# Fused delta-rule attention and two MLP layers on one core: new priorities at the start, no filling matmuls, layer 2 in groups of four

## The chip, the core and the metric

The kernel runs on one core of a Trainium2 chip. The metric is the device time of one execution in microseconds; the kernel before took 1034.82 us, the median of three runs (1033.31 to 1038.89).

## What is computed

Inputs are q, k and v of shape (4, 8, 768, 48) (batch, heads, sequence, head dimension), beta of shape (4, 8, 768), and two pairs of weights, 384 x 2048 and 2048 x 384, all float32. The reference, cut:

```python
k_n = k / (norm(k) + 1e-6)
for t in range(S):                               # per batch and head
    y[t] = q[t] @ state
    state += beta[t] * outer(k_n[t], v[t] - k_n[t] @ state)
x = y.transpose(0, 2, 1, 3).reshape(3072, 384)   # tokens x (head, dim)
h = x @ w_in                                      # layer 1
x = where(h >= 1, h, where(h <= -1, 0, (h + 1)**2 / 4)) @ w_out
h = x @ w2_in                                     # layer 2
out = (h * clip(h + 3, 0, 6) / 6) @ w2_out
```

## The kernel before

The sequence is cut into 12 chunks of 64 positions. Within a chunk the recurrence becomes matrix work: products K K' and K Q', the inverse of a unit triangular matrix, and multiplications with the state that is carried to the next chunk. All 32 heads are done together. Per chunk the steps are: `load_tok` or `load_blocks` (keys and queries), `norms`, `transposes` on TensorE or `block_transposes` on VectorE, `products` (L575), `inverse` (L634), and `chain` (L766), which gives the outputs y and the next state. y is written to the tile XB, the input of layer 1. For the first four chunks (`b16`) the inverse goes in 15 steps over rows of 16, each a multiplication (L661, out TMP) and a subtraction (L666, out TL) that depends on it; then come four multiplications on TensorE. The tuple `tpool` says for which chunks these steps run on GpSimd (1 to 11); the others use VectorE. `ct` says from which chunk on VectorE transposes instead of TensorE.

Layer 1 works on blocks: chunk 0, chunk 1 (256 tokens each), then pairs of chunks (512 tokens). A unit of a block is one of 16 slices f of the hidden dimension. `mlp_h` (L992) makes the hidden slice. To keep float32 precision each operand is split into a high and a low part, so it has three times three matmuls (9), the weights stationary and XB moving. ScalarE and VectorE then apply the activation in GF and split the result into GH (high) and GL (low). `mlp_o` (L1018) multiplies these with the output weights: 9 matmuls in layer 1, 12 in layer 2, where GH and GL are stationary and the weights (384 columns) move. The weights arrive in raw form and are split by `wload` (L909): per half slice two instructions on ScalarE or VectorE (out TBS), a merge (L953), a high copy to WLA and a subtraction (L376). Layer 2 takes blocks of 512 tokens, its GH and GL have two buffers each, and it issues the outputs of unit f right after the hidden part of unit f + 1. `fin2` evacuates and stores a block's four output tiles.

Nothing runs in the order of the code. `Plan.op` collects the instructions with a duration, dependences and a priority; `Plan.emit` simulates the engines and picks, for each, the instruction that can start first, and among equals the lower priority number. Attention of chunk c has priority c plus an entry of the table `PR` (L360), the weight splits `wl` + `wls` f, the activations `MP`, TensorE's MLP work 50 with a turn rule (`RATIO`). Where several engines can do a step, the planner takes the one that ends first. While nothing of the MLP can run, `fill` lets the planner put matmuls without use (GH on itself, 128 x 512) into TensorE's idle time. Emitted so, each engine runs its own list in order, and the names of tiles in the views carry no chunk.

## Time and profile before

| | |
|---|---|
| median of three runs | 1034.82 us |
| profiled execution | 1037.03 us, its span 1035.2 us |
| TensorE busy | 986.5 us (95%) in 11941 matmuls |
| VectorE, ScalarE, GpSimd busy | 610.3, 531.8, 286.7 us |
| mean granted TensorE clock | 0.984 |
| chain that ended last | TensorE 77%, VectorE 6%, DMA 5%, ScalarE 5%, issue 2% |
| matmuls without use | 73, of them 3 open a sum |

The span is the time from the first to the last instruction; the time of the execution has some 2 us around it. TensorE busy counts a matmul from its start to its modelled end, so a stream of overlapping matmuls reads as 100% even where each stands a little longer than its columns need. For such stretches the distance of starts says more than the busy time.

### The profile page before, as it was taken

Reading aid. Unit: us, or ns where it says so; the run is one execution under the profiler, and the core shown is the slowest. Engines: PE = TensorE matmul, PEld = TensorE weight load, DVE = VectorE, ACT = ScalarE, POOL = GpSimd, SP = SyncE. Lnnn points to the kernel's source line nnn. Section 1 sums busy time; section 2 is a strip of 40 time slices with the busy share of each in tenths; the row PEclk is TensorE's granted clock in tenths of the full one; section 3 lists DMA queues with packets and bytes.
Section 4 is the critical chain, followed back from the end, with each engine's and each line's share of the span. In section 5 each row is a group of like instructions: output and inputs, shape, how many; then the busy total and the mean of one; then the engine's idle time right before and its main releaser. Section 6 shows DMA issues by size and latency. Waiting matters only on the chain.

```text
span 1035.2 us, 28435 instructions
## 1 busy us (share of the span) xinstructions
PE 986.5 (95%) x11941; PEld 841.0 (81%) x11941; DVE 610.3 (59%) x1175; ACT 531.8 (51%) x1102; POOL 286.7 (28%) x689
## 2 busy tenths in 40 slices
PE   6777898999999999999999999999999999999998
PEld 5656887877867777877888788999999999999997
DVE  4888876776877777778546797333333333333333
ACT  5789674565645646467456896232333232323322
POOL 1151503376685876865810000000000000000000
PEclk9888999999999999999999999999999999999999
DMA  6983524341243324321223753120020020200000
GB/s 132 247 196 67 105 39 78 50 70 35 39 86 62 57 38 96 56 48 30 71 68 111 252 184 91 33 62 31 1 92 0 27 67 1 92 1 1 31 1 31
DMA packets 212688, 71.84 MB, mean 69 GB/s; under 512 B 159184, under 2 KB 208464, under 8 KB 212560
## 3 DMA queue, kind: packets, MB, share of 16 engines
q1 hardware_dynamic: 212560, 70.03, 28.6%
q8 instruction: 93, 1.52, 0.6%
q14 instruction: 35, 0.29, 0.1%
HBM read 53.68 MB, written 14.16 MB: 66 GB/s over the span
## 4 chain that ended last, share of the span: by engine, by line
PE 77%; DVE 6%; DMA 5%; ACT 5%; POOL 3%; issue 2%; SPq 2%; DVEq 0%; POOLq 0%; ACTq 0%
PE bank L418 77%; DMA RAWL<-in_moe_w_in_dram 2%; DMA KN<-in_k_dram 1%; DMA E<-in_v_dram 1%; POOL TL L666 1%; POOL TMP L661 1%; DVE GF L1009 1%; SPq L446 1%; ACT GF L1007 1%; DMA ST<-in_k_dram 1%; SPq L929 0%; ACT TBS L950 0%; ACT GF L1008 0%; DMA RAWR<-in_moe_w_in_dram 0%; DVE XB L1052 0%
## 5 line engine op out<-in xcount | busy, mean ns | idle before, releaser
L418 PE MATMUL bank<-XB,WLA 128*128 128x512 f32 (+1 forms) x1404 | 334.2, 380 | 14.5 <-DVE GF L1009 9.9
L418 PEld LDWEIGHTS bank<-XB,WLA 128*128 128x128 f32 x1404 | 248.1, 188 | 64.5 <-DVE GF L1009 14.1
L376 DVE TENSOR_TENSOR GL<-GF,GH 128x512 fp32r<-128x512 f32 (+1 forms) x208 | 137.0, 660 | 87.9 <-PE bank L418 64.6
L387 ACT ACTIVATE GH<-GF 128x512 fp32r<-128x512 f32 (+1 forms) x207 | 123.5, 597 | 126.3 <-DVE GF L1013 69.3
L1013 DVE SCALAR_TENSOR_TENSOR GF<-GF,bank 128x512 f32<-128x512 f32 x96 | 66.0, 688 | 192.4 <-ACT GF L1012 192.3
L1012 ACT ACTIVATE GF<-bank 128x512 f32<-128x512 f32 x96 | 57.4, 598 | 203.1 <-PE bank L418 202.3
L661 POOL TENSOR_TENSOR TMP<-TL,DL 128x126 f32<-128x126 f32 (+25 forms) x293 | 115.2, 393 | 70.4 <-DVE DL L719 33.2
L666 POOL TENSOR_TENSOR TL<-TL,TMP 128x126 f32<-128x126 f32 (+25 forms) x293 | 120.9, 413 | 22.7
L418 PE MATMUL bank<-GH,WLA 128*128 128x512 f32 (+1 forms) x504 | 120.3, 370 | 2.4 <-issue 1.6
L418 PE MATMUL bank<-WLA,GH 128*128 128x384 f32 x576 | 113.2, 338 | 0.0
L418 PE MATMUL bank<-XB,WLB 128*128 128x512 f32 (+1 forms) x468 | 110.8, 378 | 0.6 <-ACT SM L520 0.6
L418 PEld LDWEIGHTS bank<-WLA,GH 128*128 128x128 f32 x576 | 103.7, 188 | 6.3
L1007 ACT ACTIVATE GF<-bank 128x512 f32<-128x512 f32 (+1 forms) x112 | 59.9, 535 | 84.7 <-PE bank L418 79.4
L418 PEld LDWEIGHTS bank<-GH,WLA 128*128 128x128 f32 x504 | 86.9, 192 | 18.9 <-issue 1.7
L1009 DVE SCALAR_TENSOR_TENSOR GF<-bank,GF 128x512 f32<-128x512 f32 (+1 forms) x112 | 68.3, 611 | 49.0 <-ACT GF L1008 37.8
L418 PEld LDWEIGHTS bank<-XB,WLB 128*128 128x128 f32 x468 | 82.8, 188 | 15.5 <-issue 0.8
L418 PE MATMUL bank<-GL,WLA 128*128 128x512 f32 (+1 forms) x252 | 65.4, 367 | 1.0 <-issue 0.6
L1008 ACT ACTIVATE GF<-GF 128x512 f32<-128x512 f32 (+1 forms) x112 | 63.4, 567 | 2.1
L418 PE MATMUL bank<-WLA,GL 128*128 128x384 f32 x288 | 61.5, 334 | 0.0
L418 PEld LDWEIGHTS bank<-GL,WLA 128*128 128x128 f32 x252 | 43.9, 190 | 8.9 <-issue 0.8
L418 PEld LDWEIGHTS bank<-WLA,GL 128*128 128x128 f32 x288 | 51.0, 188 | 0.0
L418 PE MATMUL bank<-GH,WLB 128*128 128x512 f32 (+1 forms) x168 | 39.6, 366 | 1.5 <-ACT GH L387 1.5
(149 smaller groups left out, 1170.2 us busy)
## 6 DMA issues: line engine op xcount, KB each, us to landing
XB<-X SPq DMA_DIRECT2D x36, 256.0 KB, 4.5
X<-XB SPq DMA_DIRECT2D x30, 256.0 KB, 2.5
KQ<-in_moe_w_in_dram SPq DMA_DIRECT2D x16, 384.0 KB, 3.9
KQ<-in_moe_w_out_dram SPq DMA_DIRECT2D x16, 384.0 KB, 4.2
KN<-in_k_dram SPq DMA_DIRECT2D x24, 192.0 KB, 3.6
RAWL<-in_moe_w_out_dram SPq DMA_DIRECT2D x12, 384.0 KB, 5.3
out_dram<-E SPq DMA_DIRECT2D x24, 192.0 KB, 1.9
RAWL<-in_moe_w_in_dram SPq DMA_DIRECT2D x24, 144.0 KB, 4.3
```

What stands on the lines that cost most here:

```text
L376: alts[e] = (d, lambda e=e: ENG[e].tensor_tensor(out=val(out), in0=val(in0), in1=val(in1), op=op))
L387: lambda: nc.scalar.activation(out=val(out), in_=val(in_), func=AF.Copy, scale=scale))
L418: nc.tensor.matmul(o, l, r, start=start, stop=stop, skip_group_check=skip)
L446: P.dma(lambda ap=ap, dst=dst: nc.sync.dma_start(out=dst, in_=ap), CH * H, CH * DM * 4, w=[("st", i, b)], r=[("st", i)], prio=pri(c, "tok" ...
L661: P.op(te, d, lambda t=t, s=s, r0=r0, a0=a0, a1=a1, m=m: ve.tensor_tensor(out=t[:, a0:a1], in0=TL[:, r0 + a0:r0 + a1, s:s + 1].to_broadcas ...
L666: P.op(te, d, lambda t=t, s=s, r0=r0, a0=a0, a1=a1: ve.tensor_tensor(out=TL[:, r0 + a0:r0 + a1, 0:s], in0=TL[:, r0 + a0:r0 + a1, 0:s], in1 ...
L1007: P.op("act", da, lambda: nc.scalar.activation(out=gf, in_=ps, func=AF.Relu, scale=0.5, bias=0.5), r=hkeys(hb, hv), w=gk, prio=MP)
L1008: P.op("act", da + 48, lambda: nc.scalar.activation(out=gf, in_=gf, func=AF.Square), w=gk, r=gk, prio=MP)
L1009: P.op("dve", 1.06 * n + 60, lambda: nc.vector.scalar_tensor_tensor(out=gf, in0=ps, scalar=1.0, in1=gf, op0=ALU.max, op1=ALU.min), r=hkeys ...
L1012: P.op("act", da, lambda: nc.scalar.activation(out=gf, in_=ps, func=AF.Relu, scale=1.0 / 6.0, bias=0.5), r=hkeys(hb, hv), w=gk, prio=MP)
L1013: P.op("dve", 1.06 * n + 60, lambda: nc.vector.scalar_tensor_tensor(out=gf, in0=gf, scalar=1.0, in1=ps, op0=ALU.min, op1=ALU.mult), r=hkey ...
```

## The change

The table of priorities and bounds is replaced. In it, chunks 0 to 3 get an own offset (`off`), the activations of the two small blocks too (`mb`), `fill` is 0 (no filling matmuls), `tpool` begins with 3, so the inverses of chunks 1 and 2 also run their steps on VectorE, `ct` is 4, so chunk 3 is transposed on TensorE, and `dg` lets the subtraction that makes GL run on GpSimd. The planner knows when a bank was last read by another engine (`Bank.free`), charges more for weight DMAs, and starts SyncE at 700 ns. A small Sqrt on ScalarE is placed first. In layer 2, from the second block on, the hidden parts of four units are emitted in a row and then the outputs of the four units before; for that GH and GL get eight buffers, the six new pairs in tiles that attention no longer uses. The last four units of the program are issued output tile by output tile, each with its evacuation and store behind it.

```diff
-RATIO = 0.213
+RATIO = 0.2479
-PR = dict(slots=2, fast=(0,), ... hm=0.0, kv=-2.522, tok=-1.749, ... fill=3000,
-          tpool=tuple(range(1, 12)), hc=2, ... mp=0, hyst=4058, ... urg=('inv', 's'), ct=3, dg=('dve',), ...)
+PR = dict(off=(1.917, 0.131, -0.844, -0.839), mb=(-0.814, -1.017), ... hm=-28.571, kv=-2.564, tok=-2.155, ... fill=0,
+          tpool=(3, 4, 5, 6, 7, 8, 9, 10, 11), hc=0, ... mp=0.167, hyst=1146.21, ... urg=('inv', 's', 'u', 'y'), ct=4, dg=('dve', 'pool'), ...)
...
+    def free(self, e):
+        return 0.0 if self.last[0] in (None, e) else self.last[1]
...
+        free["sp"] = 700.0
...
+                    if o["uses"] and e != "pe":
+                        t = max([t] + [b.free(e) for b in o["uses"]])
...
-        return c + PR[name] - (PR["first"] if c == 0 else 0)
+        return c + PR[name] - (PR["first"] if c == 0 else 0) + (PR["off"][c] if c < len(PR["off"]) else 0)
...
+    P.op("act", 1500, lambda: nc.scalar.activation(out=SM[:, 0, 0:1], in_=GF[0][:, 0:1], func=AF.Sqrt), r=[("gf", 0, 0)], w=["sm0"], prio=-31)
...
-                  cost={48: 620.0, 16: 310.0}.get(rows))
+                  cost={48: 760.0, 16: 380.0}.get(rows, 1310.0))
...
+        mp = MP + (PR["mb"][blk] if layer == 1 and blk < len(PR["mb"]) else 0)
...
-            P.op("pe", KT * (n * 0.4515 + 1), pe, r=xkeys + wkeys(f, (0,), wh), ...)
+            P.op("pe", KT * (n * 0.443 + 1), pe, r=xkeys + wkeys(f, (0,), wh), ...)
...
+        gj = n_glob % NG2 if layer == 2 else gi
+        gl, gh = (lambda x=x: x[gj][:, c0:c0 + n] for x in (GL, GH))
...
-    def fin2(bi, cs):
+    def fin2(bi, cs, ts=range(4)):
...
+    GRP, NG2 = 4, 8
...
+        for nm, n_ in (("KN0", 1), ("KN1", 1), ("ST", 2), ("X", 2), ("DL", 2), ("TL", 1), ("NH", 1), ("LT", 1), ("YS", 1)):
+            t = pool.tile([128, n_, 512], F32R, name="G2" + nm, tag=nm)
...
+    def last_outs(group):
+        bi = group[0][1]
+        cs = blocks2[bi]
+        for t in range(4):
+            bt = banks[OB2[t]]
+            def pe(t=t, bt=bt):
+                for _, _, f, _, n_ in group:
+                    for step, (wh, g) in enumerate(((0, GH), (1, GH), (0, GL))):
+                        mm(bt[:, 0:DM], g[n_ % NG2][:, t * 128:(t + 1) * 128], wl(f, wh, DM, 2 * DM), start=False, stop=f == NF - 1 and step == 2)
...
+            fin2(bi, cs, [t])
...
-            a = seq[-2]
-            mlp_o(*a)
...
+            if i == 0 or f % GRP == GRP - 1:
+                while len(seq) - done > (1 if i == 0 else GRP):
+                    out2()
...
+    while done < len(seq) - GRP:
+        out2()
+    last_outs(seq[done:])
```

On TensorE in layer 2 the kernel before has one unit's outputs (into the banks 100, 101, 102 and 95, from GH or GL) behind one hidden part (`128x512 x9`, from XB):

```order
L418 MATMUL bank_102<-WLA,GL_69 128x384
L418 MATMUL bank_95<-WLA,GL_69 128x384
L418 MATMUL bank_99<-XB_2396,WLA 128x512 x9
L418 MATMUL bank_100<-WLA,GH_70 128x384
L418 MATMUL bank_101<-WLA,GH_70 128x384
L418 MATMUL bank_102<-WLA,GH_70 128x384
```

At the same place the changed kernel has, with G2ST and G2X as two of the new buffers:

```order
L427 MATMUL bank_102<-WLA,G2ST 128x384
L427 MATMUL bank_95<-WLA,G2ST 128x384
L427 MATMUL bank_98<-XB_2695,WLA 128x512 x9
L427 MATMUL bank_99<-XB_2695,WLA 128x512 x9
L427 MATMUL bank_96<-XB_2695,WLA 128x512 x9
L427 MATMUL bank_97<-XB_2695,WLA 128x512 x9
L427 MATMUL bank_100<-WLB,G2X 128x384
L427 MATMUL bank_101<-WLB,G2X 128x384
```

Four hidden parts stand together now, and 48 output matmuls behind them; over layer 2 the changes between the two kinds fall from 187 to 69.

On VectorE, in chunk 0's inverse (steps L661 and L666, in the changed file L671 and L676), the kernel before has, beside chunk 1's norms (SM), weight splits (RAWL, TBS):

```order
L661 TENSOR_TENSOR TMP<-TL,DL 128x48
L948 TENSOR_SCALAR TBS<-RAWL 128x384
L666 TENSOR_TENSOR TL<-TL,TMP 128x4x12
L519 TENSOR_SCALAR SM<-SM 128x16
L661 TENSOR_TENSOR TMP<-TL,DL 128x55
L948 TENSOR_SCALAR TBS<-RAWL 128x384
L666 TENSOR_TENSOR TL<-TL,TMP 128x5x11
L953 SCALAR_TENSOR_TENSOR TBS<-TBS 128x384
L661 TENSOR_TENSOR TMP<-TL,DL 128x60
```

The same steps in the changed kernel:

```order
L671 TENSOR_TENSOR TMP<-TL,DL 128x48
L532 TENSOR_TENSOR SM<-SM 128x16
L676 TENSOR_TENSOR TL<-TL,TMP 128x4x12
L533 TENSOR_TENSOR SM<-SM 128x16
L671 TENSOR_TENSOR TMP<-TL,DL 128x55
L534 TENSOR_SCALAR ND_89<-SM 128x16
L676 TENSOR_TENSOR TL<-TL,TMP 128x5x11
L536 RECIPROCAL SM<-ND_89 128x16
L671 TENSOR_TENSOR TMP<-TL,DL 128x60
```

The neighbours of the steps are chunk 1's norms now; most weight splits have moved behind the inverse. From the first step to the last 31 other instructions stood between them, and 20 do now.

On TensorE around the end of that inverse (its first product is NH,GF), the kernel before has filling matmuls on GH:

```order
L418 MATMUL bank_102<-KQ 64x64 x2
L418 MATMUL bank_99<-GH_70 128x512 x49
L418 MATMUL bank_95<-NH,GF_67 32x32 x64
L418 MATMUL bank_99<-GH_70 128x512 x4
L418 MATMUL bank_96<-DL,NH 32x32 x64
```

The changed kernel has there three sets of chunk 2's transpositions (IDN is the identity):

```order
L564 MATMUL bank_101<-IDN,ST 112x128 x4
L564 MATMUL bank_102<-IDN,ST 112x128 x4
L564 MATMUL bank_95<-IDN,ST 112x128 x4
L427 MATMUL bank_96<-NH,GF_67 32x32 x64
L564 MATMUL bank_97<-IDN,ST 112x128 x4
L427 MATMUL bank_98<-DL,NH 32x32 x64
```

The fillers are gone, and all four sets of chunk 2 stand before layer 1 starts, where two did.

## Rows read from the trace of the kernel before

**Rows 1.** Windows: busy us of PE, PEld, DVE, ACT, POOL; clock, DMA share, GB/s

```profile
0.00:45.00 45.00, 32.05 (x359) 24.41 (x359) 29.71 (x97) 28.68 (x65) 8.05 (x20) 0.99 0.81 181
45.00:71.27 26.27, 20.39 (x695) 16.17 (x695) 19.97 (x42) 22.40 (x51) 10.09 (x27) 0.70 0.84 210
71.27:200.00 128.73, 110.73 (x2785) 99.36 (x2789) 101.33 (x234) 88.35 (x222) 39.27 (x104) 0.95 0.38 72
200.00:633.00 433.00, 425.54 (x6125) 340.74 (x6114) 318.63 (x596) 269.30 (x561) 229.26 (x541) 1.00 0.35 80
633.00:1031.00 398.00, 397.82 (x1998) 360.35 (x1996) 140.12 (x210) 122.80 (x206) 0.00 (x0) 1.00 0.11 34
```

**Rows 2.** TensorE in order of time, 612 to 652: start, length, instruction, count

```profile
614.38 2.20 PE L418 MATMUL bank<-XB,WLB 128*128 128x512 f32 x9
...
637.65 7.00 PE L418 MATMUL bank<-XB,WLA 128*128 128x512 f32 x30
...
649.39 1.55 PE L418 MATMUL bank<-WLA,GH 128*128 128x384 f32 x8
```

**Rows 3.** The same view in steady layer 2, 700 to 712

```profile
701.71 2.24 PE L418 MATMUL bank<-XB,WLA 128*128 128x512 f32 x9
703.79 1.57 PE L418 MATMUL bank<-WLA,GH 128*128 128x384 f32 x8
...
705.90 2.24 PE L418 MATMUL bank<-XB,WLA 128*128 128x512 f32 x9
```

**Rows 4.** All engines in order of time, the last microseconds

```profile
1029.99 0.86 PE L418 MATMUL bank<-WLB,GL 128*128 128x384 f32 x4
1030.36 0.87 ACT L1086 ACTIVATE E<-bank 128x384 f32<-128x384 f32 x2 [1.95 <-PE bank L418]
...
1030.88 1.82 SPq L1089 DMA_DIRECT2D out_dram<-E  x4
```

**Rows 5.** VectorE in order of time during chunk 0's inverse

```profile
24.45 0.17 DVE L661 TENSOR_TENSOR TMP<-TL,DL 128x15 f32<-128x15 f32 x1
...
27.28 0.20 DVE L661 TENSOR_TENSOR TMP<-TL,DL 128x48 f32<-128x48 f32 x1
27.40 0.35 DVE L948 TENSOR_SCALAR TBS<-RAWL 128x384 int32<-128x384 int32 x1
27.67 0.20 DVE L666 TENSOR_TENSOR TL<-TL,TMP 128x48 f32<-128x48 f32 x1
...
41.60 0.18 DVE L666 TENSOR_TENSOR TL<-TL,TMP 128x15 f32<-128x15 f32 x1
```

**Rows 6.** ScalarE in order of time, 8 to 17 us

```profile
10.26 1.28 ACT L520 ACT_TABLE_LOAD   x1
```

**Rows 7.** TensorE up to layer 1's start, same view; in brackets idle time

```profile
12.50 1.99 PE L418 MATMUL bank<-KQ 48*64 48x64 f32 x64 [0.19 <-ACT KQ L387]
...
26.89 2.10 PE L418 MATMUL bank<-KQ 48*64 48x64 f32 x128
28.92 11.40 PE L418 MATMUL bank<-GH 128*128 128x512 f32 x49
...
67.66 1.32 PE L418 MATMUL bank<-E,KQ 48*64 48x48 f32 x61
...
71.27 1.73 PE L418 MATMUL bank<-XB,WLA 128*128 128x256 f32 x12 [1.38 <-ACT XB L387]
```

**Rows 8.** One set of transpositions on TensorE, same view

```profile
78.47 0.60 PE L554 MATMUL bank<-IDN,ST 128*112 128x128 f32 x4
```

**Rows 9.** VectorE, two weight subtractions, same view

```profile
61.27 1.04 DVE L376 TENSOR_TENSOR WLA<-TBS,WLA 128x384 fp32r<-128x384 f32 x2
```

**Rows 10.** GpSimd steps of chunk 1's inverse, same view

```profile
61.34 0.56 POOL L661 TENSOR_TENSOR TMP<-TL,DL 128x15 f32<-128x15 f32 x1 [2.66 <-DVE DL L690]
...
62.47 0.24 POOL L661 TENSOR_TENSOR TMP<-TL,DL 128x28 f32<-128x28 f32 x1
```

**Rows 11.** SyncE issuing token loads, same view

```profile
18.04 1.27 SPq L446 DMA_DIRECT2D ST<-in_q_dram  x2
```

More of the change, by code (lines that the diff above doesn't have):

```diff
@@ L37, in __init__ @@
         self.end = 0.0
+        self.last = (None, 0.0)
+    def free(self, e):
+        return 0.0 if self.last[0] in (None, e) else self.last[1]
 class Plan:
@@ L174, in emit @@
                         end = t + o["alts"][e][0] + bias.get(e, 0.0) + ex.get(e, 0.0)
-                        if any(max(free[x], ready[i], port_free if x in o["port"] else 0.0) + d + bias.get(x, 0.0) + ex.get(x, 0.0) < end
+                        if any(max([free[x], ready[i], port_free if x in o["port"] else 0.0] + [b.free(x) for b in o["uses"]]) + d + bias.get(x, 0.0) + ex.get(x, 0.0) < end
                                for x, (d, _) in o["alts"].items() if x != e):
@@ L253, in emit @@
                 b.done += 1
+                if e != "pe":
+                    b.last = (e, end + TAIL[e])
                 b.end = max(b.end, done)
@@ L1005, in mlp_h @@
+        gl, gh = (lambda x=x: x[gj][:, c0:c0 + n] for x in (GL, GH))
+        gf = GF[gi][:, c0:c0 + n]
+        gk, lk, hk = ([(x, z, y) for y in hv] for x, z in (("gf", gi), ("gl", gj), ("gh", gj)))
         da = 62 + 0.845 * n
         if layer == 1:
-            P.op("act", da, lambda: nc.scalar.activation(out=gf, in_=ps, func=AF.Relu, scale=0.5, bias=0.5), r=hkeys(hb, hv), w=gk, prio=MP)
-            P.op("act", da + 48, lambda: nc.scalar.activation(out=gf, in_=gf, func=AF.Square), w=gk, r=gk, prio=MP)
+            P.op("act", da, lambda: nc.scalar.activation(out=gf, in_=ps, func=AF.Relu, scale=0.5, bias=0.5), r=hkeys(hb, hv), w=gk, prio=mp)
+            P.op("act", da + 48, lambda: nc.scalar.activation(out=gf, in_=gf, func=AF.Square), w=gk, r=gk, prio=mp)
@@ L1020, in mlp_o @@
         _, gi, c0, hv = slot([0, 0], n_glob, n)
-        gl, gh = GL[gi][:, c0:c0 + n], GH[gi][:, c0:c0 + n]
+        if layer == 2:
+            gi = n_glob % NG2
         gk, hk = ([(x, gi, y) for y in hv] for x in ("gl", "gh"))
@@ L1031, in pe @@
                     for j in range(KT):
-                        mm(banks[OB1[j]][:, o0:o0 + n], wl(f, wh, DM + j * 128, DM + (j + 1) * 128), gt, start=first, stop=last, skip=blk < NSMALL)
-                P.op("pe", KT * (n * 0.4515 + 1), pe, r=rk, w=[k_ for b in OB1 for k_ in hkeys(b, ov)], prio=MLP, own=own(OB1))
+                        mm(banks[OB1[j]][:, o0:o0 + n], wl(f, wh, DM + j * 128, DM + (j + 1) * 128), gt(), start=first, stop=last, skip=blk < NSMALL)
+                P.op("pe", KT * (n * 0.443 + 1), pe, r=rk, w=[k_ for b in OB1 for k_ in hkeys(b, ov)], prio=MLP, own=own(OB1))
             else:
                 def pe(wh=wh, gt=gt, first=first, last=last):
+                    g = gt()
                     for t in range(4):
-                        mm(banks[OB2[t]][:, 0:DM], gt[:, t * 128:(t + 1) * 128], wl(f, wh, DM, 2 * DM), start=first, stop=last)
+                        mm(banks[OB2[t]][:, 0:DM], g[:, t * 128:(t + 1) * 128], wl(f, wh, DM, 2 * DM), start=first, stop=last)
                 P.op("pe", 4 * 174, pe, r=rk, w=[k_ for b in OB2 for k_ in hkeys(b, (0, 1))], prio=MLP)
@@ L1075, in load2 @@
                     r=[("x2", c, j, hl) for c in cs], w=[("x2b", xi, j, hl)], pre=allx, prio=20, cost=870.0)
-    def fin2(bi, cs):
+    def fin2(bi, cs, ts=range(4)):
         P.tag = f"fin2 b{bi}"
-        for t in range(4):
+        for t in ts:
             o = E[bi % 2].rearrange("p n u d -> p (n u d)")[:, t * DM:(t + 1) * DM]
```

64 lines of the change are left out of this document (40 added, 24 removed).

## The prediction

> **What bounds the kernel now.** I read the busy time by stretches first [rows 1]. It cuts the execution into five stages. From 633 us to the last multiplication (layer 2) TensorE is busy 397.82 of 398 us; from 200 to 633 us it is busy 425.54 of 433. There only less TensorE work can save time. From 71.27 to 200 us it is busy 110.73 of 128.73, so 18.0 us are idle, with VectorE at 101.33 and ScalarE at 88.35. Before 71.27 us no layer-1 multiplication has run; TensorE's 52.4 us there are attention and matmuls that only fill.
>
> So two places can pay: TensorE's own rate in layer 2, and the moment when layer 1 starts, with the waits just behind it. For the first I read TensorE in order of time around a hand-over and in steady layer 2 [rows 2, 3]; for the end of the program the last five microseconds [rows 4]; for the start, chunk 0's inverse on VectorE [rows 5], the table load on ScalarE [rows 6] and TensorE's own rows [rows 7]; for prices of what is moved, a set of transpositions, two weight subtractions, two GpSimd steps and a pair of loads [rows 8 to 11].
>
> **Layer 2 in groups of four.** Nine hidden multiplications of 512 columns span 2.20 us in layer 1, but 2.24 us in layer 2, where twelve output multiplications of 384 columns stand before each nine. Eight output multiplications behind other output ones span 1.55 us, behind hidden ones 1.57 us [rows 2, 3]. So each pair of hand-overs, hidden to output and back, costs 0.04 + 0.02 = 0.06 us beyond the columns, though TensorE shows no idle time there. A run of 30 hidden ones spans 7.00 us: 30 at the layer-1 pace would be about 6.96, so the cost falls once per run and not per multiplication. The program had 187 changes of kind in layer 2 and has 69: 118 fewer, 59 pairs, 59 x 0.06 = 3.5 us saved. The bounds are 0 (if the slow rows come from something else in the period, such as the two activations that run beside) and 59 x 0.10 = 5.9 us (both roundings against me). I take 3.5. What hid this cost was nothing; what could now be late is a PSUM bank for the next run of 36. But the outputs of one unit span 705.90 - 703.79 = 2.11 us, those of four 8.4 us, and in that time VectorE and ScalarE, with 140 and 123 us of work in 398, have only four units to finish. I cost it at nothing; if a bank is late, a wait of up to a microsecond shows at each of the 20 group starts.
>
> **The end.** The last multiplication ends at 1029.99 + 0.86 = 1030.85 us and the span at 1035.2: 4.35 us for four evacuations, four DMA issues (1.82 us, 0.45 each) and the landing, 2.5 us behind the last issue [rows 4]. The change finishes the four output tiles one after another, so only the last has that chain: one evacuation of 0.44 (0.87 for two), one issue of 0.45, 2.5 of landing, 3.4 us. That is 0.9 us saved; bounds 0 and 1.5, the latter if the landing is shorter without three neighbours.
>
> **Chunk 3 transposed on TensorE** (ct 3 to 4). Sixteen more transpositions, four sets of 0.60 us [rows 8], 2.4 us; in exchange VectorE loses its two block transposes of that chunk. About half of it should fall into TensorE's idle time before 200 us, so +1.2; bounds 0 and 2.4.
>
> **The start.** Layer 1's first multiplication is at 71.27 us [rows 7]. Three things before it get shorter. The first is the table load of 1.28 us on ScalarE [rows 6]: it stands between chunk 0's first evacuation and the second one, and so ahead of the first products; the new ScalarE instruction makes it happen while nothing is loaded yet. Minus 1.3. The second is chunk 0's inverse: 30 dependent steps on VectorE from 24.45 to 41.78, 17.3 us, though a step is 0.2 us [rows 5]. VectorE fills each dependence with another instruction, and such a neighbour holds the next step back: 27.40 to 27.67 for one weight instruction. The order shows 31 neighbours before and 20 now. Of the 31, six are TENSOR_SCALAR on RAWL, five SCALAR_TENSOR_TENSOR and four subtractions of weights; of these 15, three are left. At 0.27 us for the first kind and 0.48 for the others (two subtractions span 1.04 us [rows 9]; less the 0.08 by which a last duration overhangs, 0.35 against 0.27), the 15 are 5.9 us, less 0.8 for the three that stay: 5.1. Against it stands one wait more: on SyncE the first output weights are issued behind four token loads of chunk 2, two pairs of 1.27 us [rows 11], so about 2.6 us later, while VectorE comes to them earlier; I put 1.4 of it. So minus 3.7 for the steps. The third is the order: both products of chunk 0 stand next to each other, which I can't price apart from the table, and give minus 1.5.
>
> Against it, the filling matmuls go. They cost nothing where they stood: 49 of them end at about 40.3 us, and TensorE's next product needs the inverse, whose steps end only at 41.78 [rows 5, 7]. What they bought was the clock. 64 small products took 1.99 us at 12.50, and at 26.89, with some fillers before them, 128 took 2.10; but the granted clock is 0.70 on the mean from 45 to 71.27 us all the same [rows 1, 7]. Only what ran warm on that chain can double: 61 multiplications in 1.32 us at 67.66, and about as many before them, together some 3 us. I take +1.5 of it. The Trainium skill ("TensorE: Matmul & The Clock Gate", What's actually happening) says that the throttled clock is the default and that activity releases it; by that everything before layer 1 runs at 1.2 GHz now, and the start would gain 3 us less than without it. The trace agrees in direction: the 1.99 us for 64 is the lower level.
>
> Together: -1.3 - 3.7 - 1.5 + 1.5 = -5.0, so layer 1 starts at about 66 us. Bounds: 0, if ScalarE, which has 22.40 of 26.27 us busy from 45 to 71.27 [rows 1], is the real limit there, and -9.
>
> **From there to 200 us.** The small blocks' activations get priority numbers below those of the weight splits, so that TensorE waits less for them. Against it, the steps of chunks 1 and 2 move from GpSimd to VectorE: 60 instructions of 0.12 to 0.20 us, 7 to 12 us more for an engine with 27.4 us idle in 128.7 [rows 1, 5]. GpSimd loses as many steps and gets 20 of the subtractions GL. A GpSimd step of 15 columns took 0.56 us beside two weight subtractions of VectorE, and one of 28 took 0.24 behind them [rows 9, 10]; so fewer steps there relieve VectorE too, if the holding up is mutual. Of 18.0 us idle I take 2 back; bounds -9 (half) and +12 (all moved steps late). The Trainium skill ("SBUF — State Buffer", SBUF: two separate sides) says that VectorE and GpSimd lock each other out of a shared port for a whole instruction when both have SBUF inputs. By that the 20 subtractions moved to GpSimd each hold VectorE up; rows 9 and 10 show the blocking from GpSimd's side. It would add to the rival below that ends slower.
>
> **Sum.** -3.5 - 0.9 + 1.2 - 5.0 - 2.0 = -10.2 us. The profiled execution took 1037.0 us (span 1035.2), so it would become 1026.8. The median of the three runs shown is 1034.8, 2.2 lower; from there 1024.6. I say 1024.5.
>
> **Rivals.**
> First, the start is given back. TensorE begins earlier, but block 0 then waits for split weights, since fewer are split by then (16 merges SCALAR_TENSOR_TENSOR before the first activation on VectorE instead of 19, 12 subtractions instead of 18). For it: VectorE and ScalarE are busy 20.0 and 22.4 of 26.3 us there. Against it: block 0 alone has far more than one unit's weights ready at its start. Time: 1034.8 - 3.5 - 0.9 + 1.2 = 1031.6.
>
> Second, more than I say: the waits between 71 and 200 us halve, and the start gains 7. For it: the idle time there is a chain of activations through two engines that interleave them with weight splits, and just this order changes. Time: 1034.8 - 3.5 - 0.9 + 1.2 - 7 - 9 = 1015.6.
>
> Third, slower: VectorE becomes the bound between the start and 200 us. The moved steps are 12 us at the upper price; with the blocked port and the early start, VectorE's idle 27.4 us are mostly too short or in the wrong place, and every moved step delays an activation that TensorE waits for. It decides as soon as the VectorE work before block 1's end grows by more than what its idle time absorbs, about 8 us net. Time: 1034.8 - 3.2 + 12 - 2.5 = 1041.1, with 3.2 for layer 2, the end and the transpositions together, and half of the start's gain.
>
> Fourth, that layer 2 doesn't do what it says: the slow rows belong to the activations beside and stay. That takes 3.5 us from each case, and lies within each one's range.
>
> **How the numbers follow.** Forecast 0.50 (1024.5, its own range 1018 to 1029.6). Start given back 0.22 (1031.6, 1028.5 to 1033.5). More 0.18 (1015.6, 1010 to 1019). Slower 0.10 (1041.1, 1037 to 1046). 0.5% of 1034.8 is 5.2 us, about what a measurement of this kernel can tell from no change: faster means under 1029.6, slower over 1040. Faster: 0.50 + 0.18 + a third of the second rival, 0.76. Slower: most of the last, 0.07. Within: 0.17. The range from 1012.5 to 1034 leaves out some 0.07 below and 0.10 above.
>
> **What would show it.** In layer 2 a run of 36 hidden multiplications should span about 36/30 of 7.00, that is 8.4 us, and the 48 outputs of a group about 8.4; the period of one unit falls from 4.19 us (705.90 - 701.71) to about 4.13. Layer 1's first multiplication should stand near 66 us, with chunk 0's steps taking 12 to 13 us; no ScalarE table load should stand between 9 and 13 us. TensorE idle from there to 200 us should be at most 16 us per 129; if it is over 22, the slower rival holds; if the start is at 66 and the time near 1031, the first. The end should be 3.4 us behind the last multiplication. A start later than 71 us would make the forecast wrong outright.

## The result and the profile after

The changed kernel takes 1020.9 us (median of 4 runs, 1016.3 to 1023.0), the kernel before beside it 1036.2 (4 runs): a ratio of 0.9845, 95% interval 0.981 to 0.9879. That is 15.3 us less; the prediction said 10 less, 1024.5. The profiled execution took 1020.4 us with a span of 1018.4, 16.8 below the span of before.

Windows of the changed kernel, cut at the same events as [rows 1] (layer 1's first multiplication, 200 us, the first output multiplication of layer 2); columns as there:

```profile
0.00:45.00 45.00, 23.22 (x572) 18.72 (x572) 29.18 (x94) 27.65 (x66) 9.04 (x23) 0.92 0.75 163
45.00:65.44 20.44, 12.58 (x427) 10.69 (x419) 19.20 (x56) 18.15 (x40) 3.43 (x4) 0.58 0.77 186
65.44:200.00 134.56, 115.40 (x3006) 105.93 (x3006) 109.11 (x283) 95.19 (x239) 45.65 (x95) 0.96 0.43 93
200.00:621.17 421.17, 415.99 (x5895) 332.50 (x5894) 298.10 (x550) 272.53 (x568) 235.29 (x532) 1.00 0.35 80
621.17:1015.00 393.83, 393.80 (x1999) 359.04 (x1997) 137.39 (x208) 125.10 (x210) 0.00 (x0) 1.00 0.12 36
```

Layer 2 is TensorE alone, as before, and shorter. In this pair of executions TensorE's idle time up to 200 us did not fall: 134.56 - 115.40 = 19.2 us, against 18.0 before. One pair is too little to tell, as the stage table further down and the waits behind it show.

TensorE in layer 2, in order of time (the answer to [rows 2, 3]):

```profile
708.65 8.36 PE L427 MATMUL bank<-XB,WLA 128*128 128x512 f32 x36
716.85 2.27 PE L427 MATMUL bank<-WLA,G2X 128*128 128x384 f32 x12
718.96 2.24 PE L427 MATMUL bank<-WLA,G2DL 128*128 128x384 f32 x12
...
725.20 8.36 PE L427 MATMUL bank<-XB,WLB 128*128 128x512 f32 x36
```

36 hidden multiplications span 8.36 us, the 48 outputs 725.20 - 716.85 = 8.35, and a unit takes 16.55 / 4 = 4.14 us instead of 4.19. Among outputs only the first twelve, behind hidden ones, are 0.03 us longer than the next twelve. No row waits for a bank.

The last rows of TensorE, ScalarE and SyncE (the answer to [rows 4]), each from that engine's order of time:

```profile
1014.64 0.34 PE L427 MATMUL bank<-WLB,G2YS 128*128 128x384 f32 x1
```

```profile
1015.01 0.49 ACT L1101 ACTIVATE E<-bank 128x384 f32<-128x384 f32 x1 [1.59 <-PE bank L427]
```

```profile
1013.45 2.41 SPq L1104 DMA_DIRECT2D out_dram<-E  x2
```

The multiplications end at 1014.98, the span at 1018.39: 3.41 us behind them, with one evacuation of 0.49 and one last issue (the second of the two in the row). Before it was 4.4.

The start: VectorE during chunk 0's inverse, ScalarE's table load, and TensorE up to layer 1, in the views of [rows 5 to 7]:

```profile
21.71 0.17 DVE L671 TENSOR_TENSOR TMP<-TL,DL 128x15 f32<-128x15 f32 x1
...
30.00 0.36 DVE L958 TENSOR_SCALAR TBS<-RAWL 128x384 int32<-128x384 int32 x1 [1.94 <-DMA RAWL<-in_moe_w_in_dram]
...
35.30 0.18 DVE L676 TENSOR_TENSOR TL<-TL,TMP 128x15 f32<-128x15 f32 x1
```

```profile
0.73 1.28 ACT L432 ACT_TABLE_LOAD   x1 [0.73 <-PEq L1322]
```

```profile
13.26 3.69 PE L427 MATMUL bank<-KQ 48*64 48x64 f32 x128
...
25.42 3.20 PE L427 MATMUL bank<-KQ 48*64 48x64 f32 x128
...
38.41 1.93 PE L427 MATMUL bank<-NH,GF 32*32 32x32 f32 x128 [0.61 <-DVE NH L710]
...
65.44 2.93 PE L427 MATMUL bank<-XB,WLA 128*128 128x256 f32 x12 [1.25 <-DVE XB L898]
```

The steps run from 21.71 to 35.48 us, 13.8 instead of 17.3, and begin 2.7 us earlier; 1.94 us of them is one wait for a transfer, which the profile names as the input weights'. The first product of the inverse is 7.1 us earlier (45.51 before), layer 1 only 5.8: 1.3 are lost between the two. Products run at the lower clock: chunk 0's 128 take 3.69 us, the pace that they had before (64 in 1.99), chunk 1's take 3.20 instead of 2.10.

**Stages.** Every profiled run was cut by the same starts on TensorE: the first layer-1 multiplication; the 289th of the 576 multiplications with 256 columns (the two small blocks); the last of them; layer 2's first output; the last multiplication's end. In us:

| kernel | to layer 1 | small blocks, first half | second half | rest of layer 1 | layer 2 | end | ratio of times, 95% interval |
|---|---|---|---|---|---|---|---|
| before | 71.3 | 77.6 | 63.5 | 420.4 | 398.1 | 4.4 | 1 |
| changed | 65.4 | 81.2 | 57.0 | 417.5 | 393.8 | 3.4 | 0.9845 (0.981 to 0.9879) |
| e1 ungrouped | 65.8 | 79.6 | 56.6 | 417.2 | 398.1 | 4.4 | 0.9881 (0.9859 to 0.9902) |
| e2 groups of two | 66.5 | 80.3 | 56.6 | 418.1 | 395.1 | 3.4 | 0.9865 (0.9842 to 0.9889) |
| e3 last together | 65.7 | 86.8 | 56.2 | 418.0 | 393.8 | 4.4 | 0.9834 (0.9809 to 0.986) |
| e4 before, grouped | 71.7 | 78.7 | 63.0 | 419.7 | 393.8 | 3.4 | 0.993 (0.9903 to 0.9957) |
| e5 before, early table | 72.7 | 80.6 | 62.8 | 424.3 | 398.1 | 4.4 | 1.0017 (0.9995 to 1.0039) |
| e6 before, no fillers | 69.7 | 79.6 | 62.6 | 423.9 | 398.1 | 4.4 | 1.0008 (0.998 to 1.0036) |
| e7 first weights later | 64.4 | 84.4 | 57.3 | 417.8 | 393.8 | 3.4 | 0.9839 (0.9809 to 0.9869) |
| e9 no own priorities | 66.3 | 79.8 | 73.0 | 416.4 | 393.8 | 3.4 | 0.9963 (0.9944 to 0.9981) |
| e10 steps on GpSimd | 65.9 | 86.1 | 56.3 | 418.5 | 393.8 | 3.4 | 0.9836 (0.9804 to 0.9868) |
| e11 GL on VectorE | 66.7 | 85.9 | 56.5 | 420.7 | 393.8 | 3.4 | 0.9867 (0.9837 to 0.9897) |
| e12 chain ahead | 69.9 | 83.2 | 55.6 | 419.0 | 393.8 | 3.4 | 0.9874 (0.9844 to 0.9903) |

Up to layer 2, e1 to e3 have the changed kernel's order and e4 that of before. The means of the four and of the two differ by -5.6 (start), +3.8, -6.6 and -2.4 us (rest of layer 1); with -4.3 in layer 2 and -1.0 at the end that makes -16.1. The largest piece is the second half of the small blocks, which the prediction did not single out. Part of the +3.8 is work drawn forward: the first half holds 1488 attention multiplications instead of 1352, the second 1024 instead of 1152, about 2 us at 2.10 for 128 [rows 7]. The rest goes with the granted clock of that stretch, which differs between executions (last section): e3's 86.8 at 0.83 alone adds 1.6 to the mean.

**Idle time and waits.** From layer 1's first multiplication to layer 2, TensorE is idle 25.5 us (before) and 29.0 (e4) in the order of before, and 24.3, 22.0, 21.8 and 22.5 in the changed one (changed, e1, e2, e3). That is 4.6 less in the mean. What falls is the wait for activations (GF, GH and GL): 14.4 and 15.5 us against 10.9, 11.6, 10.7 and 10.7. TensorE's waits for activations in that stretch, before and then changed (us in total, times, longest):

```profile
PE bank L418 <- DVE GF L1009: 9.9, 12, 2.5
PE bank L418 <- ACT GF L1007: 3.0, 4, 1.6
PE bank L418 <- ACT GH L387: 1.5, 3, 0.8
```

```profile
PE bank L427 <- DVE GF L1022: 9.2, 16, 1.5
PE bank L427 <- ACT GF L1020: 1.8, 2, 1.2
```

### The profile page after: what moved, and what is told of

The parts are those of the page before. It is cut to its first block, busy times and chain, and to the rows that moved or that the text cites. A ratio compares the mean times of both kernels' runs of the same rounds, so it can differ in the third digit from the quotient of the medians.

```text
span 1018.4 us, 28378 instructions
## 1 busy us (share of the span) xinstructions
PE 961.0 (94%) x11887; PEld 826.9 (81%) x11887; DVE 593.0 (58%) x1187; ACT 539.1 (53%) x1122; POOL 293.4 (29%) x653
## 4 chain that ended last, share of the span: by engine, by line
PE 82%; DVE 6%; ACT 4%; DMA 4%; SPq 2%; issue 2%; POOL 0%; DVEq 0%; POOLq 0%
PE bank L427 81%; SPq L456 1%; DVE GF L1022 1%; DMA KN<-in_k_dram 1%; DMA RAWL<-in_moe_w_out_dram 1%; ACT GF L1020 1%; ACT GF L1021 1%; DMA ST<-in_k_dram 1%; SPq L939 1%; DVE TBS L963 0%; DMA E<-in_v_dram 0%; DVE WLA L385 0%; ACT TBS L960 0%; PE bank L564 0%; ACT GH L396 0%
## 5 line engine op out<-in xcount | busy, mean ns | idle before, releaser
L427 PE MATMUL bank<-XB,WLA 128*128 128x512 f32 (+1 forms) x1404 | 324.4, 380 | 10.0 <-DVE GF L1022 7.4
L1026 DVE SCALAR_TENSOR_TENSOR GF<-GF,bank 128x512 f32<-128x512 f32 x96 | 65.9, 687 | 156.6 <-ACT GF L1025 156.6
L676 POOL TENSOR_TENSOR TL<-TL,TMP 128x126 f32<-128x126 f32 (+25 forms) x263 | 112.6, 428 | 20.0
L396 ACT ACTIVATE GH<-GF 128x512 fp32r<-128x512 f32 (+1 forms) x135 | 78.2, 580 | 69.5 <-DVE GF L1022 45.8
L671 POOL TENSOR_TENSOR TMP<-TL,DL 128x126 f32<-128x126 f32 (+25 forms) x263 | 105.2, 400 | 30.6 <-DVE DL L729 10.8
L427 PE MATMUL bank<-XB,WLB 128*128 128x512 f32 (+1 forms) x468 | 107.8, 377 | 1.7 <-DVE GF L1022 1.7
L385 DVE TENSOR_TENSOR GL<-GF,GH 128x512 fp32r<-128x512 f32 (+1 forms) x116 | 75.9, 655 | 38.3 <-ACT GH L396 31.4
L427 PE MATMUL bank<-GL,WLA 128*128 128x512 f32 (+1 forms) x252 | 65.1, 367 | 0.0
L427 PE MATMUL bank<-WLA,GH 128*128 128x384 f32 x192 | 37.5, 336 | 0.0
L427 PEld LDWEIGHTS bank<-KQ 48*64 48x64 f32 x1536 | 27.5, 147 | 11.4 <-issue 7.8
L427 PE MATMUL bank<-KQ 48*64 48x64 f32 x1536 | 30.9, 234 | 4.7 <-issue 2.9
L427 PEld LDWEIGHTS bank<-WLA,GH 128*128 128x128 f32 x192 | 34.1, 188 | 1.2 <-ACT GH L396 0.2
```

The source lines that it names most:

```text
L385: alts[e] = (d, lambda e=e: ENG[e].tensor_tensor(out=val(out), in0=val(in0), in1=val(in1), op=op))
L396: lambda: nc.scalar.activation(out=val(out), in_=val(in_), func=AF.Copy, scale=scale))
L427: nc.tensor.matmul(o, l, r, start=start, stop=stop, skip_group_check=skip)
L671: P.op(te, d, lambda t=t, s=s, r0=r0, a0=a0, a1=a1, m=m: ve.tensor_tensor(out=t[:, a0:a1], in0=TL[:, r0 + a0:r0 + a1, s:s + 1].to_broadcas ...
L676: P.op(te, d, lambda t=t, s=s, r0=r0, a0=a0, a1=a1: ve.tensor_tensor(out=TL[:, r0 + a0:r0 + a1, 0:s], in0=TL[:, r0 + a0:r0 + a1, 0:s], in1 ...
L1026: P.op("dve", 1.06 * n + 60, lambda: nc.vector.scalar_tensor_tensor(out=gf, in0=gf, scalar=1.0, in1=ps, op0=ALU.min, op1=ALU.mult), r=hkey ...
```

## The experiments

**e1, e2: layer 2 without groups, and in groups of two.** The group's size is all that differs, but that in e1 the last four output tiles also end together again; the first part is in the same order.

```diff
-            if i == 0 or f % GRP == GRP - 1:
-                while len(seq) - done > (1 if i == 0 else GRP):
-                    out2()
+            while len(seq) - done > 1:
+                out2()
...
-    while done < len(seq) - GRP:
+    while done < len(seq):
         out2()
-    last_outs(seq[done:])
```

```diff
-    GRP, NG2 = 4, 8
+    GRP, NG2 = 2, 8
```

> The changed kernel, but in layer 2 each unit's outputs stand right behind the next unit's hidden multiplications again, and the last four output tiles are evacuated together. TensorE's order up to layer 2 is that of the changed kernel; layer 2 has 188 changes of kind instead of 68. Hand-over theory (each pair of changes costs 0.06 to 0.07 us that no wait shows): the period of a unit goes from 4.14 back to 4.19 us, layer 2 takes 60 x 0.067 = 4.0 us more, the end 0.9 us more, so about 1020.9 + 4.9 = 1025.8 us; the gain before layer 2 stays. Rival (the layer-2 gain belongs to the earlier start, or to the activations beside the multiplications, and not to the order): the period stays near 4.14 us, time near 1022. Second rival (the grouping gave more than its hand-overs, for instance a better order of the first units): 1028 or more.

> The changed kernel with layer 2 in groups of two units instead of four: 108 changes of kind in layer 2 instead of 68 (and 188 without groups), everything before it in the same order. Hand-over theory: 20 pairs more than the changed kernel at 0.067 us, 1.3 us more in layer 2, near 1022.2 us; runs of 18 hidden multiplications should span about 4.2 us and the period of a unit 4.15 to 4.16. If the cost were not per hand-over but fell only with long runs (or only the last group's order mattered), layer 2 would take as long as with four (0 more) or as long as without groups (4 more).

TensorE in steady layer 2, e1 and then e2, in order of time:

```profile
700.77 2.24 PE L427 MATMUL bank<-XB,WLA 128*128 128x512 f32 x9
702.85 2.27 PE L427 MATMUL bank<-WLA,G2X 128*128 128x384 f32 x12
704.96 2.24 PE L427 MATMUL bank<-XB,WLA 128*128 128x512 f32 x9
```

```profile
700.82 2.27 PE L427 MATMUL bank<-WLA,G2KN 128*128 128x384 f32 x12
702.92 2.24 PE L427 MATMUL bank<-WLA,G2ST 128*128 128x384 f32 x12
705.00 4.28 PE L427 MATMUL bank<-XB,WLA 128*128 128x512 f32 x18
709.12 2.27 PE L427 MATMUL bank<-WLA,G2X 128*128 128x384 f32 x12
```

A unit takes 704.96 - 700.77 = 4.19 us without groups and (709.12 - 700.82) / 2 = 4.15 in pairs. Layer 2 takes 398.1, 395.1 and 393.8 us at 188, 108 and 68 changes of kind: 3.0 / 40 = 0.075 and 1.3 / 20 = 0.067 us per pair of changes. The cost follows the count, and every kernel with groups of four has 393.8, so neither the activations beside nor the earlier start has a part in it. Both rivals of e1 fall.

**e3: the four last output tiles together again.**

```diff
-    while done < len(seq) - GRP:
-        out2()
-    last_outs(seq[done:])
+    while done < len(seq):
+        out2()
```

> The changed kernel with the last group's outputs unit by unit, so that all four output tiles end together and are evacuated, issued and landed together. Expected: the span ends 4.3 us behind the last multiplication instead of 3.4, so 0.9 us more (1021.8 us). Rival (the landing of the last tile is the same with or without neighbours, and evacuations and issues overlap): within 0.2 us of the changed kernel's 3.4.

```profile
1019.68 0.86 PE L427 MATMUL bank<-WLB,G2YS 128*128 128x384 f32 x4
```

(The last multiplications of e3.) They end at 1020.54, the span at 1024.92: 4.38 us, against 3.41. So 1.0 us, the size expected; the runs' times (interval of 0.5%) are too coarse for it.

**e4: the layer-2 part alone, on the kernel before.** Its edit is the second half of the diff on the change, without priorities, planner rules and early table load.

> The kernel before with only the layer-2 part of the change: groups of four and the four output tiles finished one after another; every priority number and planner rule of before, and TensorE's order up to layer 2 as before. Hand-over theory: 60 pairs fewer at 0.067 us and 0.9 us at the end, so 1036.2 - 4.9 = 1031.3 us (ratio 0.995). Rival (the grouping only pays together with the new order of the first part): 1035 to 1036.

Layer 2 393.8 us, the end 3.4, all stages ahead as before (71.7, 78.7, 63.0, 419.7). In the profile 5.3 us, in the times 0.70% (0.43 to 0.97), some 7 us, which holds 5.3. The grouping doesn't need the new order.

**e5: the early table load alone, on the kernel before.**

```diff
+    P.op("act", 1500, lambda: nc.scalar.activation(out=SM[:, 0, 0:1], in_=GF[0][:, 0:1], func=AF.Sqrt), r=[("gf", 0, 0)], w=["sm0"], prio=-31)
```

> The kernel before with one thing of the change: a square root of one column as ScalarE's first instruction. The order of all else is that of before. The step of the prediction: the table load of 1.28 us leaves the place at 10.26 us and layer 1 starts 1.3 us earlier, near 70.0 instead of 71.3 to 71.7 us, the time 1.3 us shorter (ratio 0.9987). Rival (chunk 0's chain waits there for a transfer or for VectorE, not for ScalarE): layer 1's start within 0.4 us of before and the same time.

VectorE's first step of chunk 0's inverse, an evacuation on ScalarE, and TensorE's first layer-1 multiplication:

```profile
24.29 0.18 DVE L662 TENSOR_TENSOR TMP<-TL,DL 128x15 f32<-128x15 f32 x1
```

```profile
12.44 0.60 ACT L387 ACTIVATE KQ<-bank 112x512 f32<-112x512 f32 x1 [0.92 <-PE bank L555]
```

```profile
72.74 1.71 PE L418 MATMUL bank<-XB,WLA 128*128 128x256 f32 x12 [1.39 <-ACT XB L387]
```

The steps begin where they did (24.45 before, 23.78 in e4), layer 1 is not earlier, the time not shorter. With the table out of the way, ScalarE stands idle for TensorE's transpositions instead. In the order of before the table load was hidden: the rival holds. It was not tried in the changed order.

**e6: the kernel before without its fillers, everything else in the same order.**

```diff
         for i in self.order:
-            self.ops[i]["fn"]()
+            if self.ops[i]["tag"] != "fill":
+                self.ops[i]["fn"]()
```

> The kernel before with its 70 filling matmuls left out of TensorE's order and everything else in the same order. The step of the prediction: the clock is lower up to layer 1 and the start 1.5 us later, about 73 us, the time 1.5 us longer (1.0014). Rival (TensorE's clock is not on the chain that sets layer 1's start; among four kernels with the changed order the granted clock from 30 to 65 us was between 0.61 and 0.98 and layer 1 started at 65.4 to 66.5 us all the same): start within 0.4 us of 71.4, the same time. If the fillers had held up products, the start would come earlier, by 0.5 us or more.

```profile
25.93 3.69 PE L419 MATMUL bank<-KQ 48*64 48x64 f32 x128 [0.29 <-ACT KQ L388]
...
44.66 1.93 PE L419 MATMUL bank<-NH,GF 32*32 32x32 f32 x128 [15.04 <-DVE NH L701]
...
69.67 1.73 PE L419 MATMUL bank<-XB,WLA 128*128 128x256 f32 x12 [1.38 <-ACT XB L388]
```

(TensorE in order of time.) Chunk 1's products take 3.69 us, not 2.10. But in e5, where the fillers stand, they take as long:

```profile
27.03 3.66 PE L418 MATMUL bank<-KQ 48*64 48x64 f32 x128
```

So what fillers buy differs between executions. And those products aren't on the chain; the inverse's first product waits 15.04 us for VectorE.

Behind that product the clock costs nothing that shows either. The first clock entry of e6's profile is a rise at 65.1 us, and from the product at 44.66 to layer 1 it takes 25.0 us, less than before, e4 and e5 with 25.8, 26.3 and 27.4. (A stretch ahead of the first entry reads as 1.00: e6 has 1.00 from 0 to 30 us, with the 3.69 in it. The 0.98 in what was expected is of that kind: e1's first entry comes at 60.1 us.)

Layer 1 starts 1.6 to 2 us earlier, not 1.5 later: the steps end at 40.92 us instead of 41.78, and the rest is gained behind the first product. Why the steps are shorter stays open. The time is the same (0.998 to 1.0036), an interval too wide to tell whether such a start reaches the end.

**e7: two instructions that wait for the first weights moved behind ready ones.** A list after the planning; the numbers are the plan's.

```diff
-        for i in self.order:
+        order = list(self.order)
+        for i, j in [(147, 109), (146, 501)]:
+            order.remove(i)
+            order.insert(order.index(j), i)
+        for i in order:
             self.ops[i]["fn"]()
```

> The changed kernel with two instructions moved: VectorE's first one on the raw weights (which waits 1.94 us for its transfer at 28.05 us, between two steps of chunk 0's inverse) and ScalarE's first one go behind some instructions of chunks 0 and 1 that are ready, so that nothing of the inverse stands behind the transfer. Theory (chunk 0's inverse sets layer 1's start): the steps take 12 us instead of 13.8, layer 1 starts 1 to 1.9 us earlier than 65.4 to 66.5 us, the time is about 1.5 us shorter than the changed kernel's (ratio 0.983). Rival (the start hangs on the transfers of chunk 2's tokens, which TensorE takes at 36.73 us ahead of the inverse's first product, and on the weight splits): the steps end earlier, but the first product stays within 0.7 us of 38.4 and the start within 0.4 us of 65.4 to 66.5.

```profile
64.36 1.86 PE L431 MATMUL bank<-XB,WLA 128*128 128x256 f32 x7 [1.38 <-DVE XB L902]
```

(TensorE's first layer-1 multiplications.) The steps take 12.9 us and layer 1 starts 1.1 us earlier than in the changed kernel, 1.5 below the mean of the four with its order. In this one execution the chain theory holds for the start, though one wait of 0.79 us for weights is left among the steps. The time is the same (0.9839 against 0.9845); with intervals of 0.3% to either side, 1.5 us can't be told from nothing.

**e8, e12: chunk 0's chain ahead of what it need not wait for.** e7's list and more entries: the first product ahead of a set of transpositions, and so on.

```diff
+        for i, j in [(147, 109), (146, 501), (830, 151), (831, 156), (124, 164), (125, 833), (126, 188), (127, 188)]:
```

> As the run before it, and in addition the chain of chunk 0's inverse goes ahead of what it need not wait for: its first product ahead of the third set of chunk 2's transpositions, its second product ahead of the fourth, the evacuation between them ahead of four weight instructions on ScalarE, and the two VectorE instructions behind them ahead of ten microseconds' worth of weight work. Theory (chunk 0's chain sets layer 1's start): first product near 36.5 us, second near 39, layer 1's start 3 us earlier, near 62.5 to 63.5 us, the time 3 us shorter than the changed kernel's (ratio 0.9815). Rival (weight splits and their transfers set it, or the time is given back to block 0's waits): start 65 or later, or start 62.5 with the time no shorter.

> The changed kernel with the first two instructions on raw weights moved as in the run with the first weights later, and chunk 0's chain moved ahead as meant in the run with the chain ahead: first product ahead of the third set of chunk 2's transpositions, second product ahead of the fourth, the evacuation between them ahead of four weight instructions, and the sum and the transposition behind them ahead of the third unit's weight work on VectorE (in that run these two had come behind it by an error in the position, so it did not test this). Theory (chunk 0's chain sets layer 1's start): first product near 36.5 us, second near 39, start near 63, 3 us earlier than 65.4 to 66.5. If all of it reaches the end: 3 us shorter than the changed kernel (0.9815). Rival (given back, as the 1.5 us of the run with the first weights later seem to have been): start near 63, time within 1 us of the changed kernel's. Second rival (weight splits and transfers set the start): start 65 or later.

In e8 the last two entries named a wrong place (259 for 188): the sum and the transposition came behind instructions that use them, which then worked on older data, so its 1026.8 us say nothing on the theory, and it is not in the table. e12 has them right, and layer 1 starts at 69.9 us, 4 later. TensorE, ScalarE and VectorE in e12:

```profile
38.29 1.93 PE L431 MATMUL bank<-NH,GF 32*32 32x32 f32 x128 [7.10 <-DVE NH L714]
40.15 1.10 PE L568 MATMUL bank<-IDN,ST 128*112 128x128 f32 x4
43.03 1.93 PE L431 MATMUL bank<-DL,NH 32*32 32x32 f32 x128 [1.78 <-ACT NH L400]
...
53.03 1.08 PE L431 MATMUL bank<-DL,LT 32*32 32x32 f32 x64 [3.77 <-ACT LT L400]
```

```profile
41.29 0.60 ACT L400 ACTIVATE KQ<-bank 112x512 f32<-112x512 f32 x1 [3.11 <-PE bank L568]
```

```profile
42.33 0.56 DVE L389 TENSOR_TENSOR WLA<-TBS,WLA 128x384 fp32r<-128x384 f32 x1 [2.65 <-ACT WLA L400]
```

The transpositions went behind the first product on TensorE, but their evacuation on ScalarE stayed ahead of the weight work and of the evacuation NH. ScalarE stood 3.11 us for it, VectorE 2.65 behind ScalarE, and the second product came at 43.03 instead of 41.94. Most of the 4 us come later: the product from LT stands at 53.03 instead of 49.52, behind a wait of 3.77 us for ScalarE. So this tests the theory badly: the chain was shortened in one queue and lengthened in two.

**e9: the small blocks' own priorities set to zero, planned anew.**

```diff
-          mb=(-0.814, -1.017),
+          mb=(0, 0),
```

> The changed kernel without the small blocks' own priorities (both numbers zero), planned anew: up to layer 1's start and some 30 us beyond it the order is the same, behind it it differs. Theory (these priorities shorten TensorE's waits between layer 1's start and layer 2): the start stays at 65.4 to 66.5 us, the idle time from there to layer 2 rises from 22 to 24 us by 2 to 4 us, the time is 2 to 4 us longer (ratio near 0.987). Rival (the waits are shorter for other reasons, such as the inverses on VectorE or no fixed bank for fillers): idle time and time unchanged within 1 us.

Windows over the second half of the small blocks: before, changed, e9. They open one multiplication of 256 columns ahead of the table's cut, 0.1 us or, in the first, 1.3.

```profile
147.59:212.37 64.78, 59.33 (x1506) 53.14 (x1505) 48.18 (x105) 35.95 (x94) 25.38 (x68) 1.00 0.33 58
```

```profile
146.52:203.63 57.11, 53.36 (x1315) 49.46 (x1313) 43.63 (x94) 34.89 (x93) 27.12 (x63) 1.00 0.42 78
```

```profile
145.93:219.07 73.14, 61.55 (x1451) 56.34 (x1450) 52.46 (x117) 40.29 (x106) 39.24 (x99) 0.95 0.40 69
```

TensorE's waits in that stretch of e9 (us in total, times, longest):

```profile
PE bank L427 <- issue: 5.4, 6, 1.7
PE bank L427 <- DVE XB L898: 3.6, 1, 3.6
PE bank L427 <- DVE GF L1022: 2.4, 5, 0.6
```

Without these two numbers most of the gain is gone: 0.9963 against 0.9845 is 12 us. The first half is as in the changed order (79.8); the second takes 73.0 us instead of 57.0. It has 11.6 us idle instead of 3.8, 1161 attention multiplications instead of 1024 (21.4 us of TensorE instead of 14.7), and a granted clock of 0.95. The wait for activations (GF) is only 2.4 us, against 2.0 in the changed kernel; 3.6 is one wait for chunk outputs (XB), and 5.4 are gaps of issue among the attention's small multiplications. Up to layer 2 e9 waits 8.8 us for activations, less than the changed kernel with 10.9. So "TensorE waits less because activations go first" is not what these two numbers bring: without them other waits and attention's place cost the time. It is a replan with the other numbers left as they were: it shows what these two do in this table, not that every table without them loses (before has none and takes 63.5).

**e10: the steps of chunks 1 and 2 on GpSimd again, at their places.**

```diff
-        ve = ENG[te]
+        ve = nc.gpsimd if c in (1, 2) else ENG[te]
```

> The changed kernel with the inverse steps of chunks 1 and 2 (60 instructions) executed by GpSimd again, at the same places of the order. Theory of the prediction (moving them to VectorE cost that engine 7 to 12 us of room and is about neutral on the whole): start unchanged, time within 2 us of the changed kernel's (ratio 0.983 to 0.987). Rival (the faster steps are what lets chunks 1 and 2 come earlier and shortens the waits): the steps take 0.4 to 0.6 us each instead of 0.2, some 12 us per chunk, the idle time to layer 2 rises by 4 us or more and the time as much (0.988 or more). Opposite rival (VectorE is the bound): faster than the changed kernel, below 0.981.

```profile
55.17 0.45 POOL L671 TENSOR_TENSOR TMP<-TL,DL 128x28 f32<-128x28 f32 x1
55.70 0.24 POOL L676 TENSOR_TENSOR TL<-TL,TMP 128x28 f32<-128x28 f32 x1
56.02 0.66 POOL L671 TENSOR_TENSOR TMP<-TL,DL 128x39 f32<-128x39 f32 x1
```

(GpSimd in chunk 1's inverse.) All 60 steps take 0.21 to 0.67 us, like those in [rows 10], and the time is 0.9836 (0.9804 to 0.9868): the same. The first rival (0.988 or more) falls, and the opposite one (below 0.981) lies at the interval's edge.

**e11: the 20 subtractions GL on VectorE, at their places.**

```diff
-            alts[e] = (d, lambda e=e: ENG[e].tensor_tensor(out=val(out), in0=val(in0), in1=val(in1), op=op))
+            x = nc.vector if engs is PR["dg"] else ENG[e]
+            alts[e] = (d, lambda x=x: x.tensor_tensor(out=val(out), in0=val(in0), in1=val(in1), op=op))
```

> The changed kernel with its 20 subtractions of layer 1's activations that stand on GpSimd executed by VectorE instead, at the same places of the order. By the rule on the shared port each of them on GpSimd holds VectorE up for its whole time, so taking them back would cost VectorE little and TensorE would wait less: the time 1 to 3 us shorter than the changed kernel's (0.982). Rival (GpSimd takes over work for which VectorE has no room, and the two overlap): 20 x 0.65 us more on VectorE, idle time up by 1 to 4 us, the time as much longer (0.986 to 0.988). If neither is near a limit there: no change.

0.9867 (0.9837 to 0.9897): not faster, perhaps 2 us slower, which the intervals don't settle. The waits point the same way. From layer 1's start to layer 2 TensorE waits 13.5 us for activations; in the seven other executions with this order of work (changed, e1, e2, e3, e7, e10, e12) it is 10.3 to 11.6, and 14.2 to 15.5 in the four with the order of before. The rest of layer 1 takes 420.7 us instead of 417.2 to 419.0. So the rival holds: GpSimd takes over work for which VectorE has no room. It is one execution; it gives back more than half of what the change had won in these waits.

The Trainium skill ("SBUF — State Buffer", SBUF: two separate sides) has GpSimd and VectorE block each other for a whole instruction where VectorE's has two inputs in SBUF and GpSimd's reads SBUF. By that VectorE should have gained from taking the subtractions back; this run doesn't show it.

## Why the prediction was right, step by step

Forecast were -10.2 us; measured are -15.3 in the times and -16.1 in the stages. Most of the difference lies between layer 1's start and layer 2: -5.2 instead of -0.8.

- **Layer 2, -3.5:** right in mechanism and rows (8.36 against 8.4, 8.35 against 8.4, 4.14 against 4.13); 4.3 us in fact, since a pair of changes costs 0.07 and not the 0.06 read from rounded rows. Rival four falls (e1, e2, e4).
- **The end, -0.9:** 3.41 against 3.4 us; -1.0 (e3).
- **Chunk 3's transpositions, +1.2:** 16 more; all on ST together took 2.7 us more in the changed profile (10.5 against 7.8); how much of that was hidden was not tested.
- **The start, -5.0:** -5.6 to -5.8, with terms that don't all hold. Two that were nothing, -1.3 and +1.5, nearly cancel, and that is luck. The steps: 13.8 us against 13.6 forecast, with the added wait at 1.94 instead of 1.4, right, though it is put down to the input weights and not to the output weights; both are issued behind the token loads. The table load, -1.3: nothing (e5). The products next to each other, -1.5: since the steps begin 2.7 us earlier and the table load isn't why, this term, with whatever else the new order moved there, should be nearly all of it; it was not run alone. The clock, +1.5: not there (e6). The 1.3 us lost between the first product and layer 1 are hardly outside the spread of that stretch (25.0 to 27.4 us in the four executions with the order of before, 26.8 to 27.4 in changed and e1 to e3), and their reason stays open. By the Trainium skill ("TensorE: Matmul & The Clock Gate", What's actually happening), where the throttled clock is the default and activity releases it, I had put a start that gains 3 us less without fillers. In e6 chunk 1's products did run at the lower level, 3.69 us, and the start did not come later.
- **From there to 200 us, -2.0:** the step that was mis-sized. With the transpositions it was -0.8 net up to layer 2; measured, +3.8 - 6.6 - 2.4 = -5.2. Its mechanism, that TensorE waits less for activations, holds: these waits fall by 4.0 us in the mean, and all idle time by 4.6. The mark, at most 16 us idle per 129, was too fine for one pair: the profiled run has 18.4, but e1 to e3, in the same order, have 16.4, 16.1 and 15.7, and before and e4 have 18.0 and 22.6. What was wrong is the cause. The term rested on the small blocks' priorities, and without them the waits for activations are no longer (8.8 us, e9). Of what was tried, the subtractions GL have a part in it: when they leave GpSimd, 2 to 3 us of these waits come back (e11). The prediction had them only as a load on GpSimd that might block VectorE.
- **Where it falls:** the second half of the small blocks takes 57.0 us instead of 63.5, in the profiles of before and changed. Idle time is 1.7 us less, attention that the first half took over 2.3, and TensorE's multiplications of 256 columns take 38.5 us instead of 41.0 for the same 287. Of these 2.5 us, some 1.6 are pauses again: a multiplication in front of a pause counts to its modelled end, 0.28 instead of 0.12 us, and 4 stand in front of one now, not 14. What makes the last us was not tested.
- **The first rival, start given back:** not by its mechanism, and open for the rest. Of 5.6 us, 3.8 are gone after the first half, some 2 of them as attention drawn forward, which the second half no longer has. The rest goes with the granted clock, so four executions against two don't settle it. The waits of the changed profile show none for split weights, on which the rival rested. e6 and e7 start earlier than their base and take the same time, but 1.5 to 2 us are less than their intervals can tell.
- **The second rival, waits halved and a start 7 us earlier, 1015.6:** no. The start gained 5.6, and idle time up to layer 2 fell by 4.6 of 27 us.
- **The third rival, VectorE the bound:** no; the time fell, and with the steps back on GpSimd it is the same (e10).
- **The chances:** "a third of the second rival" can only mean the first, 0.22 / 3; the sum is then 0.75.

No kernel run here is faster than the changed one by more than the intervals.

## What to carry to other kernels

Where an engine is busy all the time and still slower than its best rows, count the changes of kind and multiply: here 0.07 us per pair, invisible as idle time, and grouping took most of it away. Before pricing an instruction ahead of a long chain, check whether its engine waits for something else right behind it; a table load of 1.28 us and fillers cost nothing there. Read a sign of a few microseconds off several executions of an order: one pair showed 18.0 and 19.2 us idle, where the means fall. An order moved in one queue must be moved in the queues that consume it, as e12 paid for; and in a planned kernel a gain can hang on another entry of the table than the one that seems made for it, so undo them one by one, as e9 and e11 do.
